# Attention scores as products of rounded parts for batches 1 to 7, plain float32 for batch 0

## The chip, the cores and the metric

The kernel runs on one core of one Trainium2 chip. The metric is device time in microseconds (us), the median of several executions; lower is better. The engines are PE (TensorE, matmuls; its weight loads are listed as PEld), DVE (VectorE), ACT (ScalarE), POOL (GpSimd) and SP (SyncE, which here issues every DMA).

## What is computed

Sparse attention over q, k, v of shape (8 batches, 8 heads, 576 rows, 64), then a gated feed-forward network (FFN) with a 3-tap convolution along the rows:

```
scores = (1/8) * q @ k^T                       # (8, 8, 576, 576)
scores = where(scores >= rowmax - tau, scores, -1e9)
attn   = exp(scores - rowmax) / (sum + 1e-9)
x      = (attn @ v), heads side by side        # (8, 576, 512)
h      = relu(x @ w_in)                        # (8, 576, 1024)
gate   = sigmoid(conv3(h, conv_w))             # along the rows
out    = (h * gate) @ w_out                    # (8, 576, 512)
```

Scores near the threshold decide which entries stay, so they are needed at float32 accuracy. The weights come as float64.

## The kernel before

**Units.** Two heads make a pair (4 pairs a batch). The 576 rows of q are cut into four tiles of 128 and one of 64. A unit is one tile of one pair, both heads: 20 units a batch, 160 in all. Each batch is handled as two chunks, tiles 0 and 1 (`g == 0`) and tiles 2 to 4 (`g == 1`), and each chunk goes through its four pairs.

**A unit, step by step** (`unit`, L335; `transposes`, L406; `attend`, L457). The scores of a head go to a PSUM tile `ps_s` (two buffers) as two blocks of 288 keys. k lies turned in SBUF as `ks`, with keys 0 to 351 of a head on partitions 0 to 63 and keys 288 to 639 on partitions 64 to 127 (the first 64 keys are repeated at the end); q is there twice, once in each half. Each of the two matmuls of a head (L355) therefore uses one half of PE's rows. For the tile of 64 rows both heads share one `ps_s` tile, so four matmuls use four quarters. DVE takes the row maximum (L364), ACT the exponential into `em` (L370, four buffers), DVE masks and sums (L373), small instructions prepare the reciprocal (L367 to L396, DVE or POOL), and POOL normalizes `em` (L401). PE transposes `em` in blocks of 128 (L420; L444 for halves), ACT copies them to `eT` (L414, two buffers, one a pair and chunk), and PE multiplies them with v into `pa` (L466). ACT and DVE split `pa` into a rounded part and a remainder (L474, L477).

**FFN.** `mm1` (L496) and `mm2` (L561) multiply in F32R, a float32 that has been rounded for PE: every operand is a rounded part (ACT copy into an F32R tile) and a remainder (a subtraction on POOL or DVE, L227), and three products are summed. `gh` and `gl` (L540, L227) are the two parts of the FFN's hidden values.

**Preparation.** `prep` (L595) loads, for each pair, `ks` (L319, and L320 multiplies it by 1/8 on ACT; once a batch), q (L327) and v (L332). It is called at a pair's first unit, for the next pair.

**Order.** Nothing is scheduled by the compiler. Each operation is given to `Plan` with an engine, an estimated duration in ns and a rank: the number of its unit minus a lead (`AHEAD`: 4.5 units for scores, 4.0 transposes, 3.5 `pa`, 5.5 preparation and 2 more for its DMAs, 0 for the FFN). `Plan.run` (L74) plays the estimates through: an engine that is free takes the ready operation of lowest rank, provided that a buffer of its tile is free, and this order is what each engine's queue gets. An operation with `other` may go to a second engine when the first one's backlog is over `BACKLOG`. For a score block of PE the estimate is 490, for the 1/8 `act(n)` = 0.833 n + 93, for a subtraction on POOL `pool(n)` = 2.1 n + 150.

## Time and profile before

| | us |
|---|---|
| median of 3 runs | 1017.34 (1016.53 to 1019.24) |
| the profiled execution: time | 1015.53 |
| the profiled execution: span, first to last instruction | 1013.7 |
| PE busy / weight loads | 973.3 / 688.9 |
| DVE, ACT, POOL busy | 766.4, 623.1, 561.4 |

The profile is one execution. A view names an instruction by its line in the kernel (L355), engine, operation and tiles (out<-in), with the shape and the count; "idle before" is the time its engine had nothing to do just ahead of it, and the arrow names what ended that. The timeline lists instructions by start; neighbours of the same line and tiles are merged (x4), and their length is from the first start to the last end. PE's ends are modelled and overlap with the next start, so distances between starts are what to read. PE's shape 64*128 means 64 rows and 128 columns of the array.

### The profile page before, as it was taken

The numbers are of one execution on the slowest core, as the hardware profiler recorded it, in microseconds if no ns is written. First come the engines' busy times: TensorE is split into PE (matmuls) and PEld (weight loads), VectorE is DVE, ScalarE is ACT, GpSimd is POOL, SyncE is SP. The second block draws the span as 40 slices with busy tenths as digits, with TensorE's granted clock in tenths as the row PEclk, the third lists the DMA queues.
The fourth block names the chain that finished last, engine by engine and source line by source line (L and its number), as shares of the span: only waits on it lengthen the run. The fifth ranks groups of instructions, "written<-read, shape, count | busy, mean of one in ns | idle before, by whom it ended". The sixth has DMA issues, their size and how long they took to land.

```text
span 1013.7 us, 18810 instructions
## 1 busy us (share of the span) xinstructions
PE 973.3 (96%) x6368; PEld 688.9 (68%) x6368; DVE 766.4 (76%) x1984; ACT 623.1 (61%) x1375; POOL 561.4 (55%) x1028
## 2 busy tenths in 40 slices
PE   5797878999999999999999999999999999999998
PEld 3464545766777677767677767776777767777786
DVE  5989998767778678886868768977687767896543
ACT  5677675665656566666656556766565655675442
POOL 3567665644556456754556536575455645584343
PEclk9899898999999999999999999999999999999999
DMA  5434243122212212212222221221222121210000
GB/s 167 123 118 125 88 117 92 43 84 72 61 52 67 71 59 63 68 57 79 61 63 64 74 61 58 67 62 64 71 63 78 49 72 38 86 34 31 22 22 31
DMA packets 41407, 70.44 MB, mean 69 GB/s; under 512 B 3936, under 2 KB 20320, under 8 KB 41312
## 3 DMA queue, kind: packets, MB, share of 16 engines
q1 hardware_dynamic: 41312, 69.25, 22.5%
q8 instruction: 51, 0.84, 0.4%
q14 instruction: 44, 0.36, 0.1%
HBM read 59.79 MB, written 9.44 MB: 68 GB/s over the span
## 4 chain that ended last, share of the span: by engine, by line
PE 83%; DVE 8%; POOL 3%; issue 2%; ACT 2%; DMA 1%; POOLq 0%; SPq 0%; ACTq 0%; DVEq 0%
PE ph L496 20%; PE po L561 18%; PE ps_s L355 16%; PE pa L466 14%; PE ps_t L420 14%; DVE few L364 2%; DVE em L373 2%; POOL em L401 2%; DMA stage<-in_w_in_dram 1%; DVE stage L265 1%; PE ps_t L444 1%; DVE stage L269 1%; POOL gl L227 1%; DVE t L523 1%; POOL t L514 1%
## 5 line engine op out<-in xcount | busy, mean ns | idle before, releaser
L401 POOL TENSOR_SCALAR em<-em,few 128x576 f32<-128x576 f32 x288 | 260.5, 911 | 77.5 <-DVE few L396 58.2
L364 DVE TENSOR_REDUCE few<-ps_s 128x1 f32<-128x576 f32 x288 | 213.6, 751 | 110.9 <-PE ps_s L355 109.6
L370 ACT ACTIVATE em<-ps_s,few 128x576 f32<-128x576 f32 x288 | 212.1, 742 | 84.8 <-DVE few L364 70.7
L373 DVE SCALAR_TENSOR_TENSOR em<-ps_s,few,em 128x576 f32<-128x576 f32 x288 | 231.9, 812 | 34.7 <-ACT em L370 30.6
L496 PE MATMUL ph<-x,w1h 128*128 128x322 f32 (+1 forms) x1024 | 255.9, 315 | 0.0
L414 ACT ACTIVATE eT<-ps_t 128x512 f32<-128x512 f32 (+1 forms) x448 | 198.6, 477 | 74.9 <-PE ps_t L420 72.0
L355 PE MATMUL ps_s<-ks,q 64*128 64x288 f32 (+1 forms) x1280 | 207.8, 451 | 25.1 <-DVE em L373 14.9
L420 PE MATMUL ps_t<-ident,em 128*128 128x128 f32 x1280 | 206.8, 285 | 9.8 <-POOL em L401 7.7
L420 PEld LDWEIGHTS ps_t<-ident,em 128*128 128x128 f32 x1280 | 149.5, 143 | 80.6 <-issue 25.8
L496 PEld LDWEIGHTS ph<-x,w1h 128*128 128x128 f32 x1024 | 177.3, 189 | 35.9 <-issue 26.3
L523 DVE SCALAR_TENSOR_TENSOR t<-hp,cw,t 128x255 f32<-128x255 f32 (+1 forms) x256 | 157.6, 618 | 29.7 <-POOL t L514 27.1
L466 PE MATMUL pa<-eT,v 128*64 128x256 f32 (+1 forms) x1280 | 171.6, 414 | 0.4 <-ACT eT L414 0.4
L496 PE MATMUL ph<-x,w1l 128*128 128x322 f32 (+1 forms) x512 | 152.2, 297 | 0.1
L355 PEld LDWEIGHTS ps_s<-ks,q 64*128 64x128 f32 (+1 forms) x1280 | 90.6, 178 | 87.7 <-issue 42.0
L466 PEld LDWEIGHTS pa<-eT,v 128*64 128x64 f32 x1280 | 86.8, 138 | 72.7 <-issue 7.6
L227 POOL TENSOR_TENSOR gl<-t,gh 128x321 fp32r<-128x321 f32 (+13 forms) x184 | 120.2, 664 | 28.2 <-ACT gh L540 27.1
L561 PE MATMUL po<-w2h,gh 128*128 128x512 f32 x288 | 122.7, 426 | 0.7 <-ACT gh L540 0.7
L514 POOL TENSOR_SCALAR t<-hp,cw 128x321 f32<-128x321 f32 (+1 forms) x128 | 72.2, 565 | 89.8 <-ACT hp L511 85.2
L367 POOL TENSOR_SCALAR few<-few,tau_sb 128x1 f32<-128x1 f32 x106 | 39.1, 369 | 135.7 <-DVE few L364 119.7
L561 PE MATMUL po<-w2h,gl 128*128 128x512 f32 x288 | 113.7, 395 | 0.5 <-POOL gl L227 0.3
L561 PE MATMUL po<-w2l,gh 128*128 128x512 f32 x288 | 113.6, 394 | 0.2 <-POOL w2l L227 0.2
L496 PEld LDWEIGHTS ph<-x,w1l 128*128 128x128 f32 x512 | 97.0, 190 | 0.9 <-POOL w1l L227 0.5
(47 smaller groups left out, 805.9 us busy)
## 6 DMA issues: line engine op xcount, KB each, us to landing
v<-in_vc_dram SPq DMA_DIRECT2D x64, 320.0 KB, 3.0
ks<-in_kd_dram SPq DMA_DIRECT2D x32, 352.0 KB, 3.6
q<-in_qd_dram SPq DMA_DIRECT2D x32, 320.0 KB, 3.3
out_dram<-ot SPq DMA_DIRECT2D x36, 256.0 KB, 2.0
q<-in_qd_dram SPq DMA_DIRECT2D x32, 256.0 KB, 3.1
stage<-in_w_in_dram SPq DMA_DIRECT2D x16, 256.0 KB, 3.3
stage<-in_w_out_dram SPq DMA_DIRECT2D x16, 256.0 KB, 2.9
stage_c<-in_conv_w_dram SPq DMA_DIRECT2D x1, 24.0 KB, 6.8
```

The lines of the kernel that those rows point to most:

```text
L227: engines[e].tensor_tensor(dst, x, y, op=ALU.subtract)
L355: nc.tensor.matmul(ps[r * n:(r + 1) * n, c, :CH], lhsT=q[rows, j, o:o + n], rhs=k[rows, j, r * D:r * D + CH], start=True, stop=True)
L364: nc.vector.tensor_reduce(few[:rows, nm], ps[:rows, :, :CH], op=ALU.max, axis=mybir.AxisListType.XY, negate=True)
L370: nc.scalar.activation(view(), ps[:rows, :, :CH], AF.Exp, bias=few[:rows, nm])
L373: nc.vector.scalar_tensor_tensor(view(), ps[:rows, :, :CH], few[:rows, th], view(), op0=ALU.is_ge, op1=ALU.mult, accum_out=few[:rows, total])
L401: engines[e].tensor_scalar(sl, sl, few[:rows, 6 + h:7 + h], few[:rows, 8 + h:9 + h], op0=ALU.mult, op1=ALU.add)
L414: "act", act(w, True), lambda dst=dst, src=src: nc.scalar.activation(dst(), src(pt), AF.Copy),
L420: nc.tensor.transpose(out=pt[:, i * P:(i + 1) * P], in_=em[:, (b0 + i) * P:(b0 + i + 1) * P], identity=ident[:])
L466: nc.tensor.matmul(pa[j * D:(j + 1) * D, :w], lhsT=vt[:, blk + j, :], rhs=eT[:, blk, :w], start=(r == 0), stop=(r == 4))
L496: nc.tensor.matmul(ph[:, :an], lhsT=w1[w][:, cb, fs], rhs=xs[cb][:, h, :an], start=(cb == 0 and i == 0), stop=(cb == NCB - 1 and i == 2))
L523: nc.vector.scalar_tensor_tensor(t[:, :kn], hp[:, k:kn + k], cw[:, 3 * f + k:3 * f + k + 1], t[:, :kn], op0=ALU.mult, op1=ALU.add)
L561: nc.tensor.matmul(po[:], lhsT=x[:, f, at:at + P], rhs=w[:, f, :], start=(f == 0 and i == 0), stop=(f == NFB - 1 and i == 2))
```

## The change

For batch 0 (`plain(b)`) the scores stay as they are: two float32 matmuls on row halves, with k and q loaded for each head by itself.

For batches 1 to 7 each head's k is loaded whole on both halves of the partitions (576 columns for the first head of a pair, 640 for the second), multiplied by 1/8 (ACT), copied to an F32R tile, which rounds it (ACT), and in the lower half of the partitions (64 to 127) the rounded value is replaced by the remainder (POOL, or DVE). q, which lies on both halves already, is split into `q1`, rounded, and `q2`, the remainder. A matmul over all 128 rows of `q1` with `ks` then gives q1 k1 + q1 k2, one of `q2` gives q2 k1 + q2 k2, and their sum is the score: four F32R matmuls a head, two for each block of 288 keys. For the tile of 64 rows the second head is multiplied first, over 128 columns (its neighbour rows in q come along), and the first head then writes rows 0 to 63 anew with 64 columns: eight matmuls.

Beside it: `em` has 3 buffers instead of 4, `eT` 1 instead of 2; preparation is called for each head j, at the first and at the second unit of the pair before; the estimate of a score block is 700 (plain) or 560 a head; k on the host is laid out like q.

```diff
@@ -313,32 +313,74 @@
     ring = [const(f"g{i}", [P, NFB, RING], F32R) for i in "hl"]
-    def prep_k(b, p):
-        ks = plan.buf(wk, "ks", 5, [P, 2, CH + D], F32, f"ks_{b}_{p}")
-        op("sp", 1000, lambda: nc.sync.dma_start(ks[:], kd[b, p]), w=[(ks, 0)], ahead=AHEAD["prep"] + 2)
-        op("act", act(2 * (CH + D)), lambda: nc.scalar.activation(ks[:], ks[:], AF.Copy, scale=0.125), w=[(ks, 0)], ahead=AHEAD["prep"])
+    def plain(b):
+        return b == 0
+    def prep_k(b, p, j):
+        n = f"{b}_{p}_{j}"
+        w = S + j * D
+        a = AHEAD["prep"]
+        if plain(b):
+            ks = plan.buf(wk, f"ks{j}", 5, [P, w], F32, f"ks_{n}")
+            cut = CH + D
+            for c in range(2):
+                rows, at = slice(c * D, (c + 1) * D), c * CH
+                m = min(cut, w - at)
+                op(
+                    "sp", 500, lambda rows=rows, at=at, m=m: nc.sync.dma_start(ks[rows, :m], kd[b, p, rows, j, at:at + m]),
+                    w=[(ks, c)], ahead=a + 2
+                )
+            cut = CH + j * D
+            op("act", act(cut), lambda: nc.scalar.activation(ks[:, :cut], ks[:, :cut], AF.Copy, scale=0.125), w=[(ks, 0), (ks, 1)], ahead=a)
+            return ks
+        xk = plan.buf(wk, "xk", 2, [P, S + D], F32, f"xk_{n}")
+        ks = plan.buf(wk, f"ks{j}", 5, [P, w], F32R, f"ks_{n}")
+        op("sp", 820, lambda: nc.sync.dma_start(xk[:, :w], kd[b, p, :, j, :w]), w=[(xk, 0)], ahead=a + 2)
+        op("act", act(w), lambda: nc.scalar.activation(xk[:, :w], xk[:, :w], AF.Copy, scale=0.125), w=[(xk, 0)], ahead=a)
+        op("act", act(w), lambda: nc.scalar.activation(ks[:], xk[:, :w], AF.Copy), w=[(ks, 0), (ks, 1)], r=[(xk, 0)], ahead=a)
+        op(
+            "pool", pool(w), lambda e: subtract(e, ks[D:], xk[D:, :w], ks[D:].bitcast(F32)),
+            w=[(ks, 0), (ks, 1)], r=[(xk, 0)], ahead=a, other=[("dve", dve(w))]
+        )
         return ks
-    def prep_q(b, p, g):
+    def prep_q(b, p, j, g):
         o, w = NEW[g]
-        q = plan.buf(wk, "q", 3, [P, 2, w], F32, f"q_{b}_{p}_{g}")
-        op("sp", 900, lambda: nc.sync.dma_start(q[:], qd[b, p, :, :, o:o + w]), w=[(q, 0)], ahead=AHEAD["prep"] + 2)
-        return q
+        n = f"{b}_{p}_{j}_{g}"
+        src = qd[b, p, :, j, o:o + w]
+        a = AHEAD["prep"]
+        if plain(b):
+            q1 = plan.buf(wk, "q1", 4, [P, w], F32, f"q1_{n}")
+            op("sp", 455, lambda: nc.sync.dma_start(q1[:], src), w=[(q1, 0)], ahead=a + 2)
+            return [q1]
+        xq = plan.buf(wk, "xq", 2, [P, w], F32, f"xq_{n}")
+        q1 = plan.buf(wk, "q1", 4, [P, w], F32R, f"q1_{n}")
+        q2 = plan.buf(wk, "q2", 4, [P, w], F32R, f"q2_{n}")
+        op("sp", 455, lambda: nc.sync.dma_start(xq[:], src), w=[(xq, 0)], ahead=a + 2)
+        op("act", act(w), lambda: nc.scalar.activation(q1[:], xq[:], AF.Copy), w=[(q1, 0)], r=[(xq, 0)], ahead=a)
+        op(
+            "pool", pool(w), lambda e: subtract(e, q2[:], xq[:], q1[:].bitcast(F32)),
+            w=[(q2, 0)], r=[(xq, 0), (q1, 0)], ahead=a, other=[("dve", dve(w))]
+        )
+        return q1, q2
     def load_v(b, p, g):
         vt = plan.buf(wk, "v", 2, [P, NBLK + 1, D], F32, f"v_{b}_{p}_{g}")
         op("sp", 820, lambda: nc.sync.dma_start(vt[:], vc[b, p]), w=[(vt, 0)], ahead=AHEAD["prep"])
         return vt
-    def unit(u, k, q, o, n):
+    def unit(u, kt, qt, o, n):
         heads = [[0, 1]] if 2 * n <= P else [[0], [1]]
         m, rows = len(heads), n * len(heads[0])
-        em = plan.buf(wk, "em", 4, [P, 2 * S], F32, f"em_{u}")
+        em = plan.buf(wk, "em", 3, [P, 2 * S], F32, f"em_{u}")
         few = plan.buf(sm, "few", 4, [P, 10], F32, f"few_{u}")
         a = AHEAD["s"]
@@ -348,14 +390,25 @@
             nm, th, total = (slice(at + h, at + h + 1) for at in (0, 2, 4))
             def mm(js=js, ps=ps):
-                for r, j in enumerate(js):
+                if len(qt[0]) == 1:
+                    for r, j in enumerate(js):
+                        for c in range(2):
+                            on = slice(c * D, (c + 1) * D)
+                            nc.tensor.matmul(
+                                ps[r * n:(r + 1) * n, c, :CH], lhsT=qt[j][0][on, o:o + n], rhs=kt[j][on, r * D:r * D + CH],
+                                start=True, stop=True
+                            )
+                    return
+                for r, j in reversed(list(enumerate(js))):
                     for c in range(2):
-                        rows = slice(c * D, (c + 1) * D)
-                        nc.tensor.matmul(
-                            ps[r * n:(r + 1) * n, c, :CH], lhsT=q[rows, j, o:o + n], rhs=k[rows, j, r * D:r * D + CH],
-                            start=True, stop=True
-                        )
+                        at = r * D + c * CH
+                        for i in range(2):
+                            nc.tensor.matmul(
+                                ps[:(r + 1) * n, c, :CH], lhsT=qt[j][i][:, o - r * n:o + n], rhs=kt[j][:, at:at + CH],
+                                start=(i == 0), stop=(i == 1)
+                            )
             def view(h=h):
                 return em[:rows, h * S:(h + 1) * S].rearrange("p (a b) -> p a b", a=2)
@@ -376,7 +429,8 @@
                 )
             op(
-                "pe", 490, mm, w=[(ps, 0)], r=[(k, 0), (q, 0)], ahead=a
+                "pe", 560 * len(js) if len(qt[0]) > 1 else 700, mm, w=[(ps, 0)],
+                r=[(kt[j], i) for j in js for i in range(2)] + [(x, 0) for j in js for x in qt[j]], ahead=a
             )
             op("dve", 665, top, w=[(few, ("nm", h))], r=[(ps, 0)], ahead=a)
             op("act", 624, exp, w=[(em, h)], r=[(ps, 0), (few, ("nm", h))], ahead=a)
@@ -592,17 +646,19 @@
     units = [(i, t) for i in range(len(pairs)) for t in GROUPS[pairs[i][0] % 2]]
     kss, qss, vts, ems, eTs = {}, {}, {}, {}, {}
-    def prep(i):
+    def prep(i, j):
         if i >= len(pairs):
             return
         c, p = pairs[i]
         b, g = chunks[c]
         if g == 0:
-            kss[b, p] = prep_k(b, p)
-        qss[i] = prep_q(b, p, g)
-        vts[i] = load_v(b, p, g)
-    prep(0)
+            kss[b, p, j] = prep_k(b, p, j)
+        qss[i, j] = prep_q(b, p, j, g)
+        if j == 0:
+            vts[i] = load_v(b, p, g)
+    for j in range(2):
+        prep(0, j)
     load_conv()
     for i in range(W1N + W2N):
@@ -616,10 +672,10 @@
             c, p = pairs[i]
             b, g = chunks[c]
             n = TILES[t][1]
-            em = unit(now, kss[b, p], qss[i], TILES[t][0] - NEW[g][0], n)
+            em = unit(now, [kss[b, p, j] for j in range(2)], [qss[i, j] for j in range(2)], TILES[t][0] - NEW[g][0], n)
             w = NEW[g][1]
             if t == GROUPS[g][0]:
-                eT = plan.buf(wk, "eT", 2, [P, NBLK, 320], F32, f"eT_{i}")
+                eT = plan.buf(wk, "eT", 1, [P, NBLK, 320], F32, f"eT_{i}")
             transposes(now, em, n, eT, TILES[t][0] - NEW[g][0])
             if t == GROUPS[g][-1]:
                 x = plan.buf(wk, f"x{g}", NP, [P, 2, COLS[g][1]], F32R, f"x{g}_{i}")
@@ -633,7 +689,9 @@
                     )
                 attend(i, eT, vts[i], w, x, off)
             if t == GROUPS[g][0]:
-                prep(i + 1)
+                prep(i + 1, 0)
+            if t == GROUPS[g][1]:
+                prep(i + 1, 1)
             if t == GROUPS[g][-1] and p == NP - 1:
                 seq = ffn(c)
@@ -666,15 +724,13 @@
         x = np.asarray(x).reshape(B, H // 2, 2, -1, D).transpose(0, 1, 4, 2, 3)
         return np.concatenate([x, x], axis=2)
-    turned = np.concatenate([np.asarray(k), np.asarray(k)[:, :, :64]], axis=2)
-    turned = turned.reshape(B, H // 2, 2, S + 64, D).transpose(0, 1, 2, 4, 3)
     blocks = np.asarray(v).reshape(B, H // 2, 2 * S // 128, 128, D)
     middle = np.zeros((B, H // 2, 2, 128, D), np.float32)
     middle[:, :, 0, :64] = blocks[:, :, 4, :64]
     middle[:, :, 1, 64:] = blocks[:, :, 4, 64:]
     ins = {
         'qd': doubled(q),
-        'kd': np.stack([turned[..., :S // 2 + 64], turned[..., S // 2:]], axis=2).transpose(0, 1, 2, 4, 3, 5).reshape(B, H // 2, 2 * D, 2, -1),
+        'kd': doubled(np.concatenate([np.asarray(k), np.asarray(k)[:, :, :64]], axis=2)),
         'vc': np.concatenate([blocks[:, :, :4], middle, blocks[:, :, 5:]], axis=2).transpose(0, 1, 3, 2, 4),
         'tau': np.asarray(tau).reshape(1, 1),
         'w_in': np.asarray(moe_w_in).view(np.int64),
```

## The prediction

> **What bounds the kernel now.** I read the page's busy times first, then the table of windows, PE's waits in the middle window, and last the timeline of PE alone, because the score matmuls are what the change rewrites.
>
> ```profile
> span 1013.7 us, 18810 instructions
> ...
> PE 973.3 (96%) x6368; PEld 688.9 (68%) x6368; DVE 766.4 (76%) x1984; ACT 623.1 (61%) x1375; POOL 561.4 (55%) x1028
> ...
> 200.00:950.00 750.00, 748.91 (x5021) 535.35 (x5019) 567.41 (x1469) 467.55 (x1029) 415.13 (x764) 1.00 0.21 62
> ...
> PE ps_t L420 <- POOL em L401: 0.8, 3, 0.3
> PE ps_t L420 <- POOL hp L508: 0.3, 1, 0.3
> ```
>
> Columns of the third line: window, length, then busy us of PE, PEld, DVE, ACT and POOL, the granted clock (1.00), DMA share and GB/s. PE is busy 748.9 of 750 us, and the two wait rows are all that PE waited for there: 1.1 us. The other 39 of its 40.4 idle us (1013.7 - 973.3) lie before 200 us and after 950 us. In that window DVE is at 76%, ACT at 62%, POOL at 55%. So from 200 to 950 us only PE time counts; before it, PE time saved may be worth nothing.
>
> Busy does not say what a score block really takes from PE, since the matmuls overlap in their records. Starts do. Four places of PE's timeline (start, length, line, names, shape, count):
>
> ```profile
> 515.80 0.31 PE L496 MATMUL ph<-x,w1l 128*128 128x322 f32 x1
> 515.95 0.31 PE L496 MATMUL ph<-x,w1h 128*128 128x322 f32 x1
> 516.18 0.76 PE L355 MATMUL ps_s<-ks,q 64*128 64x288 f32 x4
> 516.87 0.42 PE L496 MATMUL ph<-x,w1h 128*128 128x322 f32 x1
> 517.12 0.32 PE L496 MATMUL ph<-x,w1l 128*128 128x322 f32 x1
> ```
> ```profile
> 374.59 0.28 PE L496 MATMUL ph<-x,w1h 128*128 128x256 f32 x1
> 374.71 0.60 PE L420 MATMUL ps_t<-ident,em 128*128 128x128 f32 x4
> 375.24 0.76 PE L355 MATMUL ps_s<-ks,q 64*128 64x288 f32 x4
> 375.93 0.66 PE L420 MATMUL ps_t<-ident,em 128*128 128x128 f32 x4
> 376.34 0.36 PE L496 MATMUL ph<-x,w1h 128*128 128x256 f32 x1
> ```
> ```profile
> 308.77 0.31 PE L496 MATMUL ph<-x,w1h 128*128 128x322 f32 x1
> 309.00 1.24 PE L355 MATMUL ps_s<-ks,q 64*128 64x288 f32 x8
> 310.18 0.42 PE L496 MATMUL ph<-x,w1h 128*128 128x322 f32 x1
> 310.43 0.31 PE L496 MATMUL ph<-x,w1l 128*128 128x322 f32 x1
> ```
> ```profile
> 303.34 0.31 PE L496 MATMUL ph<-x,w1h 128*128 128x322 f32 x1
> 303.58 0.71 PE L355 MATMUL ps_s<-ks,q 64*64 64x288 f32 x8
> 304.23 0.42 PE L496 MATMUL ph<-x,w1h 128*128 128x322 f32 x1
> 304.48 0.32 PE L496 MATMUL ph<-x,w1l 128*128 128x322 f32 x1
> ```
>
> The trace shows each plain float32 matmul as two records, so x4 is one head of a 128-row tile, x8 two heads, and the x8 of 64*64 both heads of a 64-row tile. Read the starts. A ph matmul of 322 columns follows another after 0.15 us (515.80 to 515.95). The last ph ahead of a score block holds PE for 0.23 (515.95 to 516.18), 0.08 more; the block of one head takes 0.69 (516.18 to 516.87); the first ph behind it takes 0.25 instead of 0.15. One head therefore costs 0.69 + 0.08 + 0.10 = 0.87 us between ph blocks. A second head in the same block adds only 0.48 (309.00 to 310.18 is 1.18, the single 0.69 with rounding). So of 0.87 us some 0.4 is the price of switching into row halves and out again. Between transposes it is much the same: four transposes ahead of the block take 0.53 (374.71 to 375.24), four behind it 0.41.
>
> **The change, part by part.** *Scores of batches 1 to 7, 128-row tiles.* Two matmuls on row halves become four over all 128 rows, in the rounded type that ph runs in. From ph's spacings, 0.12 us for 256 columns (374.59 to 374.71) and 0.15 for 322, a 288-column one takes 0.134, one head 0.54. No switch should remain: ph has the same 128*128 shape, and passing between ph and transposes costs nothing visible (the transposes start 0.12 after the ph, at its usual spacing). The saving per block:
> one head between ph: 0.87 - 0.54 = 0.33; between transposes 0.69 + 0.09 + 0.05 - 0.54, about 0.30 (0.53 against four transposes at 0.11, 0.41 against 0.36); two heads between ph: 1.18 + 0.08 + 0.10 - 1.07 = 0.29, between transposes 0.25. Beside pa less, since pa is itself of another shape (128*64):
>
> ```profile
> 509.64 2.38 PE L466 MATMUL pa<-eT,v 128*64 128x256 f32 x20
> 511.95 0.33 PE L420 MATMUL ps_t<-ident,em 128*128 128x128 f32 x1
> ```
>
> pa pays its own exit whoever follows (2.31 us for the block, before transposes as well), so a neighbouring score block shares it; I take 0.15 for one head and 0.08 for two.
>
> How many blocks lie in the saturated window:
>
> ```profile
> 200.00:950.00 750.00, 157.77 (x1016) 69.63 (x1016) 347.66 (x681) 167.26 (x227) 1.00 0.21 62
> ```
>
> These are the rows of the score tile there: 1016 matmul records, which I counted in PE's timeline as 112 blocks of one head, 44 of two and 27 of a 64-row tile (112 x 4 + 44 x 8 + 27 x 8 = 1016). That is 254 heads of 320; the 66 earlier ones are all 40 of batch 0 and 26 of batch 1, so the window is wholly changed work, and a batch takes 750 x 40 / 254 = 118 us. By neighbours: 85 singles free of pa (0.32 on average: 27.2 us), 27 beside pa or a 64-row block (0.15: 4.0), 22 pairs free (0.27: 5.9), 22 beside pa (0.08: 1.8). Sum 39 us.
>
> *64-row tiles lose.* Now both heads run at once in 64*64 quarters: 303.58 to 304.23 is 0.65, with 0.09 before and 0.10 after 0.84 us. Then there are eight full matmuls, 8 x 0.134 = 1.07: 0.23 lost. Four of the eight write 64 columns only, as pa and the quarters do; if they need the switch too, another 0.27 goes (0.09 in, 0.10 out, and a block's end of about 0.09), 0.5 in all. No row shows this shape in the rounded type; 27 x 0.23 to 0.5 is 6 to 13.5 us. I take 10: a 64-column output is what pa, the nearest row, has, but pa's switch is often shared. PE's balance: 39 - 10 = 29 us (25 to 33).
>
> *What the other engines get.* Rows of the same kind of work:
>
> ```profile
> L320 ACT ACTIVATE ks<-ks 128x704 f32<-128x704 f32 x32 | 25.3, 791 | 19.6 <-DMA ks<-in_kd_dram 19.6
> ...
> L540 ACT ACTIVATE gh<-t 128x320 fp32r<-128x320 f32 x8 | 3.7, 461 | 0.0
> L540 ACT ACTIVATE gh<-t 128x256 fp32r<-128x256 f32 x8 | 3.3, 414 | 0.0
> ...
> L227 POOL TENSOR_TENSOR gl<-t,gh 128x320 fp32r<-128x320 f32 x8 | 7.1, 889 | 0.5 <-ACT gh L540 0.5
> L227 POOL TENSOR_TENSOR gl<-t,gh 128x256 fp32r<-128x256 f32 x8 | 6.3, 794 | 0.0
> L227 POOL TENSOR_TENSOR gl<-t,gh 128x64 fp32r<-128x64 f32 x8 | 2.7, 341 | 1.6 <-ACT gh L540 1.6
> ```
>
> ACT, per batch: 4 activations of 704 go (3.2 us); for k, 8 of 576 and 8 of 640 come (0.68 and 0.74 by the slope from 320 to 704 columns: 11.4) and for q 8 of 256 and 8 of 320 (7.0): +15 us. POOL, per batch: 4 subtractions of 576, 4 of 640 (1.44 and 1.57 by the slope from 64 to 320) and 8 each of 256 and 320: 12.0 + 13.5 = +25.5 us. Over a batch of 118 - 29 / 6.35 = 113.5 us that makes ACT (467.6 / 6.35 + 15) / 113.5 = 78%, POOL (415.1 / 6.35 + 25.5) / 113.5 = 80%, DVE 567.4 / 6.35 / 113.5 = 79%. None becomes the bound by itself. All of it is hidden under PE as long as PE's order never meets a late operand; DVE at 76% leaves PE waiting 1.1 us today. Uncovered it would cost up to its own length, 6.35 x 40 us.
>
> *Cover that shrinks.* em goes from four buffers to three, eT from two to one. A unit takes 118 / 20 = 5.9 us, so three em buffers still allow 17.7 us from exp to transposes. One eT means that the next pair's transposes can't be copied out before pa has ended; at 511.95 the transposes come after pa anyway. Nothing for both, up to the price of the second rival below. The planner's prices matter more: it charges a score block 490 ns where PE needs 690 to 870, so PE runs late against the plan and everybody else comes early. The new 560 is close to 0.54. That reserve is part of why PE never waits, and it shrinks. No row prices it; between 0 and that rival's 62 us, I take 6, about 1 us a batch, nearer to zero because the row nearest to it is the 1.1 us of waiting in 750.
>
> *SP and batch 0.* SP issues 8 transfers for k and 16 for q a batch instead of 4 and 8, with v and out behind them in its one queue, and they wait for a free xk or xq. DMA share is 0.21, prep is ranked 7.5 units ahead: nothing. Batch 0 keeps its matmuls; its k comes in smaller pieces: nothing, give or take 2 us in the 200 us that PE does not fill.
>
> Sum: -29 + 6 = **-23 us**. The profiled execution took 1015.53 us (span 1013.7 and 1.8 around it); the median of the runs is 1017.34. So 992.5 against the profile and **994** against the median.
>
> **Rivals.** *The reserve is gone* (partial gain): waits of 9 to 26 us in place of my 6, 1003 to 1014. For: three engines near 80% and plan prices that now fit. Against: POOL and ACT have idle time in every unit today.
>
> *Norms come late* (slower). The norm on POOL is the last step ahead of the transposes, and it now queues behind subtractions.
>
> ```profile
> L401 POOL TENSOR_SCALAR em<-em,few 128x576 f32<-128x576 f32 x288 | 260.5, 911 | 77.5 <-DVE few L396 58.2 <-PE ps_t L420 8.7 <-PE pa L466 6.6
> ```
>
> Subtractions hold POOL 25.5 of 113.5 us, so 22% of the norms find one running, and wait for half of 1.1 us on average, or for a second one: 0.25 us for each of the 252 norms of seven batches, 62 us in all, with one em buffer fewer to absorb it. If all of it reached PE: 1017 - 29 + 62 = 1050; it decides from about half, 29 us. Against: ffn's gl work already shares that queue, and the norm's 260.5 us on POOL let 0.8 us of waiting through to PE.
>
> *The halves were worth it* (slower). If the switch belongs to plain float32 beside rounded matmuls and not to row halves, the transposes keep it alive, and only streaming is compared: 200 heads x (0.54 - 0.48) + 27 x (1.07 - 0.65) = +23 us, 1040. The Trainium skill, TensorE: Matmul & The Clock Gate, section "Why this matters for your kernels", has the same bent: it advises running small-K matmuls concurrently in separate row groups. By that rule the change gives away a factor that it should keep; the trace agrees for the second head of a block (0.48), not for a block with its ends (0.87). Against: transposes, plain float32 as well, start after ph at ph's own spacing.
>
> *No change*: gain and waits cancel within 3 us.
>
> **How the numbers follow.** Chances: forecast (982 to 1003) 0.66, partial gain (1003 to 1014) 0.13, no change 0.07, late norms 0.11, halves 0.03. 0.3% is 3 us, about what a measurement of this kernel can tell from no change. Faster 0.79, same 0.07, slower 0.14. The low end is the upper balance with no waits, 1017 - 33 = 984, and 2 for the start: 982. The high end takes in the partial gain and no change, and leaves the two slower cases out: 1018.
>
> **What would show it.** Right: score matmuls of batches 1 to 7 as x4 a head, 128*128, at 0.13 us spacing, with ph behind them at its usual 0.15; PE busy over 99% in a middle window some 25 us shorter; ACT and POOL at 76 to 82% there. Wrong: PE rows waiting for em, eT or q in the tens of us; a spacing above 0.17 in the new matmuls; 64-row tiles above 1.4 us. If the time is above 1014, a wait has taken the gain.

## The result and the profile after

The changed kernel takes 1032.07 us (median of 4 runs, 1030.21 to 1032.39); the kernel before, run beside it, 1016.93 (1016.12 to 1019.24). The ratio is 1.0141, 95% interval 1.012 to 1.0162: slower by 15 us, where 23 us faster was forecast. The profiled execution has a span of 1029.7 us against 1013.7.

The page of after (busy us, share of the span, instructions):

```profile
span 1029.7 us, 19586 instructions
...
PE 958.9 (93%) x6368; PEld 762.4 (74%) x6368; DVE 815.2 (79%) x2077; ACT 705.7 (69%) x1575; POOL 712.2 (69%) x1103
```

The windows of after, in the columns of the prediction, and then the first window of before:

```profile
0.00:200.00 200.00, 157.13 (x947) 104.34 (x948) 176.73 (x454) 136.78 (x304) 134.28 (x206) 0.91 0.39 115
...
200.00:950.00 750.00, 727.07 (x4991) 596.52 (x4990) 603.32 (x1548) 536.66 (x1195) 549.12 (x843) 1.00 0.24 71
```
```profile
0.00:200.00 200.00, 165.45 (x1027) 104.63 (x1027) 173.68 (x468) 131.86 (x288) 122.28 (x218) 0.93 0.36 111
```

PE's waits in after from 200 to 950 us (total, times, longest):

```profile
PE ps_t L474 <- POOL em L455: 16.0, 24, 1.3
PE ps_t L474 <- DVE x L531: 2.2, 5, 0.6
PE ps_s L408 <- DVE em L426: 2.1, 6, 0.7
```

PE is less busy than before (958.9 against 973.3), so the new matmuls are cheaper. But it now idles in the window that it had filled: 22.9 of 750 us, where it was 1.1. The largest wait is the transposes' for a norm on POOL, 16.0 us where it was 0.8. In the first 200 us PE does less as well (157.1 busy for 165.5, 947 matmul records for 1027), although batch 0 keeps its score matmuls.

**The new matmuls by themselves.** PE's timeline of after: a head between `ph` blocks, and a 64-row tile:

```profile
291.63 0.31 PE L550 MATMUL ph<-x,w1h 128*128 128x322 f32 x1
291.77 0.71 PE L408 MATMUL ps_s<-ks,q 128*128 128x288 f32 x4
292.32 0.32 PE L550 MATMUL ph<-x,w1h 128*128 128x322 f32 x1
292.48 0.31 PE L550 MATMUL ph<-x,w1l 128*128 128x322 f32 x1
...
315.36 0.31 PE L550 MATMUL ph<-x,w1h 128*128 128x322 f32 x1
315.51 1.22 PE L408 MATMUL ps_s<-ks,q 128*128 128x288 f32 x8
316.56 1.04 PE L474 MATMUL ps_t<-ident,em 128*128 128x128 f32 x8
```

The head takes 0.55 us (291.77 to 292.32), and the `ph` around it keep their usual 0.15: no switch is left, against 0.87 in all before. The x8 is half 128*128 and half 128*64 (timelines merge neighbours), as the view of the tile in that window shows:

```profile
L408 PE MATMUL ps_s<-ks,q x8: 292/294/296, 315.5 to 316.4; 128*128 128x288 f32 x4, 128*64 128x288 f32 x4
```

It takes 1.05 us (315.51 to 316.56), so the 64-column half pays no switch either.

**Time that PE loses.** For each pair of neighbouring matmuls I took the usual distance of their starts, and added up what exceeds it. The span less this sum is the work that PE would do unhindered.

| us | before | after |
|---|---|---|
| beyond the usual, 0 to 200 us | 51.1 | 66.0 |
| beyond the usual, from 200 us | 4.8 | 35.2 |
| span less both | 957.8 | 928.5 |

So PE's work fell by 29.3 us, and 45.3 us of loss came: 14.9 in the first 200 us, 30.4 behind them. What counts as usual moves these sums: taken over all runs and also by what stands ahead of the pair, they are 32.6 and 48.7 (16.2 and 32.5), so they are good to some 3 us. The experiments ask where these 45 us come from.

### The profile page after: what moved, and what is told of

Its sections match the earlier page's. It is cut to its first block, busy times and chain, and to the rows that moved or that the text cites. A ratio compares the mean times of both kernels' runs of the same rounds, so it can differ in the third digit from the quotient of the medians.

```text
span 1029.7 us, 19586 instructions
## 1 busy us (share of the span) xinstructions
PE 958.9 (93%) x6368; PEld 762.4 (74%) x6368; DVE 815.2 (79%) x2077; ACT 705.7 (69%) x1575; POOL 712.2 (69%) x1103
## 4 chain that ended last, share of the span: by engine, by line
PE 25%; DVE 14%; POOL 7%; ACT 4%; issue 4%; DMA 1%; POOLq 0%; ACTq 0%; DVEq 0%
PE po L615 8%; PE ps_s L408 4%; PE pa L520 4%; PE ps_t L474 4%; DVE em L426 4%; PE ph L550 4%; DVE t L577 4%; DVE few L417 3%; POOL em L455 3%; POOL gl L227 2%; DVE t L584 1%; ACT em L423 1%; POOL t L568 1%; POOL q L227 1%; ACT eT L468 1%
## 5 line engine op out<-in xcount | busy, mean ns | idle before, releaser
L455 POOL TENSOR_SCALAR em<-em,few 128x576 f32<-128x576 f32 x288 | 262.5, 918 | 66.6 <-DVE few L450 53.7
L426 DVE SCALAR_TENSOR_TENSOR em<-ps_s,few,em 128x576 f32<-128x576 f32 x288 | 231.0, 811 | 33.7 <-ACT em L423 30.9
L550 PE MATMUL ph<-x,w1h 128*128 128x322 f32 (+1 forms) x1024 | 247.0, 308 | 0.8 <-ACT hp L565 0.8
L468 ACT ACTIVATE eT<-ps_t 128x512 f32<-128x512 f32 (+1 forms) x448 | 198.8, 477 | 48.7 <-PE ps_t L474 47.1
L408 PE MATMUL ps_s<-ks,q 128*128 128x288 f32 (+1 forms) x1120 | 194.4, 307 | 10.9 <-DVE em L426 10.2
L577 DVE SCALAR_TENSOR_TENSOR t<-hp,cw,t 128x255 f32<-128x255 f32 (+1 forms) x256 | 175.7, 690 | 33.3 <-POOL t L568 18.0
L408 PEld LDWEIGHTS ps_s<-ks,q 128*128 128x128 f32 (+1 forms) x1120 | 158.8, 185 | 28.6 <-issue 11.7
L520 PE MATMUL pa<-eT,v 128*64 128x256 f32 (+1 forms) x1280 | 175.0, 421 | 0.6 <-ACT eT L468 0.6
L568 POOL TENSOR_SCALAR t<-hp,cw 128x321 f32<-128x321 f32 (+1 forms) x128 | 74.8, 585 | 58.6 <-ACT hp L565 52.6
L227 POOL TENSOR_TENSOR q<-xq,q 128x256 fp32r<-128x256 f32 (+1 forms) x112 | 93.6, 843 | 28.8 <-ACT q L365 19.6
```

The costliest lines, as they stand in the source:

```text
L227: engines[e].tensor_tensor(dst, x, y, op=ALU.subtract)
L408: nc.tensor.matmul(ps[:(r + 1) * n, c, :CH], lhsT=qt[j][i][:, o - r * n:o + n], rhs=kt[j][:, at:at + CH], start=(i == 0), stop=(i == 1))
L426: nc.vector.scalar_tensor_tensor(view(), ps[:rows, :, :CH], few[:rows, th], view(), op0=ALU.is_ge, op1=ALU.mult, accum_out=few[:rows, total])
L455: engines[e].tensor_scalar(sl, sl, few[:rows, 6 + h:7 + h], few[:rows, 8 + h:9 + h], op0=ALU.mult, op1=ALU.add)
L468: "act", act(w, True), lambda dst=dst, src=src: nc.scalar.activation(dst(), src(pt), AF.Copy),
L520: nc.tensor.matmul(pa[j * D:(j + 1) * D, :w], lhsT=vt[:, blk + j, :], rhs=eT[:, blk, :w], start=(r == 0), stop=(r == 4))
```

## The experiments

The matmul term stood. Four readings of the loss could be told apart: the smaller buffers; the new *order* (a plan with more work in it); POOL's *time* (its norms queue behind the subtractions); and *holding* (a POOL instruction that runs keeps a DVE instruction from finishing, or the other way round). All ratios are to the kernel before, with their 95% interval. Lines differ between kernels: the tap of the convolution is L523 before and L577 after, the gate L530 and L584, the norm L401 and L455.

### Buffers alone, in the kernel before (b_buf)

```diff
-        em = plan.buf(wk, "em", 4, [P, 2 * S], F32, f"em_{u}")
+        em = plan.buf(wk, "em", 3, [P, 2 * S], F32, f"em_{u}")
...
-                eT = plan.buf(wk, "eT", 2, [P, NBLK, 320], F32, f"eT_{i}")
+                eT = plan.buf(wk, "eT", 1, [P, NBLK, 320], F32, f"eT_{i}")
```

> The kernel before with em at 3 buffers and eT at 1, nothing else. Theory A (the subtractions on POOL delay the norms and hold up VectorE): the buffers are not the cause, 1017 +- 4 us, PE waits from 200 to 950 us stay under 5 us. Theory B (the smaller buffers take the cover away): PE waits for transposes as in the changed kernel; most of the 45 us of added PE waits appears without the 29 us saved in matmuls, 1040 to 1062 us. Theory C (the planner's new prices and a plan that now fits too tightly): 1017 +- 4.

1017.03 us, 1.0005 (0.9993 to 1.0017). In the kernel before, the buffers cost nothing.

### The subtractions as a load on the kernel before (b_load)

For batches 1 to 7, subtractions of the change's sizes into scratch; the scores stay as they are.

```diff
+        if b:
+            for j in range(2):
+                n = S + j * D
+                dk = plan.buf(wk, "dk", 1, [P, S + D], F32R, f"dk_{b}_{p}_{j}")
...
+                op("pool", pool(n), load, w=[(dk, 0)], r=[(ks, 0)], ahead=AHEAD["prep"], other=[("dve", dve(n))])
```

> The kernel before with added work that nothing reads: for batches 1 to 7 the same 168 subtractions on POOL as in the change (64 partitions by 576 and 640 columns for k, 128 by 256 and 320 for q), from ks and q into a scratch tile, at the same rank. Scores stay plain float32. Theory A: VectorE's instructions with two operands from SBUF get longer (taps of 321 columns from 646 to about 740 ns on average), norms come late, PE waits; since PE is slower than in the changed kernel part is absorbed: 1025 to 1045. Theory B and C: POOL has room (55 to 73 percent busy), 1017 +- 4.

1039.83 us, 1.0223 (1.0203 to 1.0244). The added subtractions alone cost 23 us without the new matmuls, though they take 149 us of POOL where the change's take 181. Most of it is lost early: the score matmul that starts at 225 us before starts 17.5 us later here, and the last ones 25 us later. Behind that PE, with its dearer score blocks, waits hardly more than before (0.7 us for norms from 200 to 930).

### The change without subtractions (a_nosub)

Both subtractions are gone: k's lower half stays rounded and q's rounded part is used twice, so the remainders are left out of the scores (and the rounded product counts four times).

```diff
-        op(
-            "pool", pool(w), lambda e: subtract(e, ks[D:], xk[D:, :w], ks[D:].bitcast(F32)),
-            w=[(ks, 0), (ks, 1)], r=[(xk, 0)], ahead=a, other=[("dve", dve(w))]
-        )
...
-        return q1, q2
+        return q1, q1
```

> The changed kernel without the subtractions: k keeps its rounded value in both halves and q's rounded part is used in place of its remainder, so the remainders are left out of the scores; matmuls, loads, ACT copies, buffers and prices stay. Theory A: PE's waits go and the matmuls' gain shows, 985 to 998. Theory B: waits stay, 1025 to 1032. Theory C: POOL's part goes but the tight plan stays, 1010 to 1025.

988.72 us, 0.9721 (0.9701 to 0.9742): the forecast without its 6 us of waits (1017 - 29 = 988). Everything else that the change does (ACT's added work, SP's transfers, the buffers, the plan's new prices) costs nothing that shows. The whole loss hangs on the subtractions.

### All subtractions on DVE (a_dve)

```diff
-            "pool", pool(w), lambda e: subtract(e, ks[D:], xk[D:, :w], ks[D:].bitcast(F32)),
-            w=[(ks, 0), (ks, 1)], r=[(xk, 0)], ahead=a, other=[("dve", dve(w))]
+            "dve", dve(w), lambda: subtract("dve", ks[D:], xk[D:, :w], ks[D:].bitcast(F32)),
+            w=[(ks, 0), (ks, 1)], r=[(xk, 0)], ahead=a
```

(and the same for q)

> The changed kernel with all subtractions given to VectorE. Theory A: POOL's norms are on time again, but VectorE gets 14 us a batch more (about 90 percent busy) and its two-operand work still meets POOL's; the early stretch, where VectorE is full, loses more: 1025 to 1045. Theory B: norms do not matter, the smaller buffers do: 1030 +- 5, about the changed kernel. Theory C: 1030 to 1045.

1027.8 us, 1.0108 (1.009 to 1.0126), with DVE busy 628.2 of 730 us from 200 to 930. Moving the work changes little: PE's transposes still wait 15.2 us for norms there, presumably because DVE's maxima and sums, which the norms need, now stand behind the subtractions.

### One-operand load on the kernel before (b_load1)

As b_load, with multiplications by 1 in place of the subtractions, sized to hold POOL about as long (158 us in all, for 149):

```diff
-                    subtract(e, dk[D:, :n], x, x)
+                    m = {576: 524, 640: 605}[n]
+                    for _ in range(2):
+                        engines[e].tensor_scalar(dk[D:, :m], x[:, :m], 1.0, 1.0, op0=ALU.mult, op1=ALU.mult)
```

> The kernel before with the same occupation of POOL as in the run with 168 added subtractions, at the same ranks and planned costs, but from instructions with one tensor operand and constants (multiplications by 1 into a scratch tile that nothing reads). Theory A1 (VectorE's instructions with two SBUF operands cannot run beside POOL's with two): no exclusion, so VectorE's taps keep their length and the time stays at 1017 to 1022. Theory A2 (the norms queue behind the added work on POOL, whatever it is): the loss of 23 us stays, 1035 to 1042.

1033.7 us, 1.0164 (1.0144 to 1.0185). It was meant to keep POOL's time and take the holding away, and did not: taps that begin beside such a multiplication are longer by the time it has left, less 0.2 us (correlation 0.98 and 1.0 for k's and q's). One operand holds DVE as two do, so this run separates nothing.

### Subtractions in pieces (a_split)

```diff
+        for i in range(4):
+            at = slice(i * w // 4, (i + 1) * w // 4)
+            op(
+                "pool", pool(w // 4), lambda e, at=at: subtract(e, ks[D:, at], xk[D:, at], ks[D:, at].bitcast(F32)),
+                w=[(ks, i % 2)], r=[(xk, 0)], ahead=a, other=[("dve", dve(w // 4))]
+            )
```

(q in two pieces likewise)

> The changed kernel with each subtraction for k in four pieces and each for q in two, on the same engine; the work is the same plus a fixed 0.15 us for each of the 280 added instructions. A1: what VectorE waits for is the rest of the running piece, at most 0.5 instead of 1.5 us; of the 45 us of added waits a third to a half goes, 1010 to 1022. A2: POOL has 42 us more work and nothing gets better, 1030 to 1040.

1023.62 us, 1.0071 (1.005 to 1.0092): 8 us better than after. Presumably shorter instructions let norms in between and hold DVE for less; the pieces' own starts raise POOL's busy time from 712 to 759 us.

### No subtraction for k (a_nosubk)

k's remainder is left out; q is split as in the change.

> The changed kernel without the subtractions for k: both halves keep k's rounded part, so k's remainders are left out of the scores; q is still split. Waits for a running instruction go with the square of its length: 56 of 1.43 and 1.57 us against 112 of 0.79 and 0.89 us is 126 to 79. A1: some 60 percent of the 43 us between the changed kernel and the one without subtractions comes back, 1002 to 1010. A2 goes by the time held, 86 to 94 us: about half, 1008 to 1014.

1001.86 us, 0.9861 (0.9833 to 0.9888). k's subtractions account for 30 of the 43 us between this series' ends (988.7 and 1032.1), q's for the other 13, though they hold POOL for about as long. POOL's groups in after:

```profile
L227 POOL TENSOR_TENSOR ks<-xk,ks 64x640 fp32r<-64x640 f32 x28 | 46.0, 1641 | 2.0
L227 POOL TENSOR_TENSOR ks<-xk,ks 64x576 fp32r<-64x576 f32 x28 | 41.7, 1488 | 4.6 <-ACT ks L344 2.4
L227 POOL TENSOR_TENSOR q<-xq,q 128x320 fp32r<-128x320 f32 x56 | 50.0, 900 | 18.9 <-ACT q L365 9.8 <-PE ps_s L408 8.0 <-DVE few L450 0.8
L227 POOL TENSOR_TENSOR q<-xq,q 128x256 fp32r<-128x256 f32 x56 | 43.6, 786 | 9.9 <-ACT q L365 9.8
```

k: 87.7 us in 56 instructions of 1.5 to 1.6 us; q: 93.6 us in 112 of 0.8 to 0.9. The long ones cost more than their share, with one reservation: k was removed first, while both loads were there, and the second of two loads may cost more than the first.

### Batches 0 and 1 plain (a_plain2)

```diff
-        return b == 0
+        return b <= 1
```

> The changed kernel with batches 0 and 1 plain instead of batch 0 alone. By the starts of the scores, 14 us of the loss arise before 250 us, while VectorE is full with the weights, and none after. If the subtractions for batch 1 meet the weights there, 1016 to 1023; if the early loss comes from smaller buffers or prices, 1030 +- 3.

1021.83 us, 1.0046 (1.0029 to 1.0062), 10 us better than after. In the first 250 us, where the weights are prepared on the same engines, the subtractions buy less than they cost.

### POOL held by memsets, kernel before (b_memset)

As b_load, with memsets in place of the subtractions (169 us on POOL, for 149). A memset reads nothing.

```diff
-                    subtract(e, dk[D:, :n], x, x)
+                    for m in (640, 640) if n == 576 else (640, 640, 180):
+                        engines[e].memset(dk[:, :m], 0.0)
```

> The kernel before with POOL held for about the same time as in the two runs with added work, at the same ranks and planned costs, but by memsets of a scratch tile, which read nothing. A1 (VectorE's two-operand instructions wait for POOL's running instruction): memsets of one column showed no such wait before; if longer ones show none either, taps of 321 columns stay near 650 ns and the time is 1017 to 1022. A2 (the added work delays POOL's own work, the norms): 1033 to 1040 as with the other added work.

1031.43 us, 1.0135 (1.0091 to 1.0179). Taps beside a memset are not longer (-2 and -4 ns in the middle of 10 and 33 cases), so a load that doesn't hold DVE exists. It costs 14 us here, b_load 23: the taps came out as A1 has it, the time nearer to A2's.

### The added operations in the plan alone, kernel before (b_noop)

As b_memset, with memsets of one column and the plan's prices kept: the order stays, POOL's time goes.

```diff
-                    for m in (640, 640) if n == 576 else (640, 640, 180):
+                    for m in (1,):
```

> The kernel before with the added operations of the earlier load runs still in the plan at full planned cost, but each issuing only a memset of one column. So every engine's order is that of the load runs, and POOL's time is not. O (the changed order in the early stretch costs the time): 1028 to 1034, as with the memsets. A2 (POOL's time itself, its own work comes late): 1017 +- 4.

1021.08 us, 1.0039 (1.0025 to 1.0052). With b_memset and b_load, the kernel before pays some 4 us for the order, 10 for POOL's time, 9 for the holding. The last two are good to 5 us only: b_memset's four runs lie between 1026 and 1037 us, and it kept POOL busy for 20 us more than b_load.

### The order of the change alone (a_noop)

Subtractions of one column, at their full price in the plan; q's rounded part is used twice, so the remainders are left out.

```diff
-            "pool", pool(w), lambda e: subtract(e, ks[D:], xk[D:, :w], ks[D:].bitcast(F32)),
+            "pool", pool(w), lambda e: subtract(e, ks[D:, :1], xk[D:, :1], ks[D:, :1].bitcast(F32)),
...
-            "pool", pool(w), lambda e: subtract(e, q2[:], xq[:], q1[:].bitcast(F32)),
+            "pool", pool(w), lambda e: subtract(e, q2[:, :1], xq[:, :1], q1[:, :1].bitcast(F32)),
```

> The changed kernel with its order kept: the subtractions are planned at full cost but work on one column; the scores take q's rounded part twice, so the remainders are left out. O: the early loss of some 14 us stays and the waits after 200 us go, 1000 to 1005. A1 and A2: all of the 43 us goes, as without subtractions, 986 to 992.

986.45 us, 0.9702 (0.9684 to 0.972). In the changed kernel the order costs nothing, nor do the 38.5 us that the one-column subtractions still take on POOL.

### The order and POOL's time, without the holding (a_memset)

Memsets in the subtractions' places, 177 us in all for their 181; the remainders are zeros.

```diff
-            "pool", pool(w), lambda e: subtract(e, ks[D:], xk[D:, :w], ks[D:].bitcast(F32)),
+            "pool", pool(w), lambda e: [engines[e].memset(ks[D:, :m].bitcast(F32), 0.0) for m in (w, w, 200 if w == S else 330)],
```

(and the same for q with `(w, w, w // 6)`)

> The changed kernel in its own order, with memsets in place of the subtractions that hold POOL for about the same time (0.75 to 1.6 us each); the remainders are then zero, so they are left out of the scores. Long memsets did not lengthen VectorE's taps. A1 (exclusion of VectorE): PE's waits from 200 to 950 us fall from 33 to about 10, 1003 to 1012. A2 (POOL's own work comes late): the waits stay near 30, 1025 to 1033.

1008.0 us, 0.991 (0.9892 to 0.9927). That splits the loss. From a_noop to a_memset the ratio rises by 0.0208, 21 us: POOL's time. From a_memset to after by 0.0231, 24 us: the holding. Together 45 us, all of it; each part is good to some 3 us. The windows from 200 to 930 us, of a_noop, a_memset and after:

```profile
200.00:930.00 730.00, 726.11 (x5054) 604.79 (x5054) 571.81 (x1549) 537.94 (x1196) 420.17 (x834) 1.00 0.24 71
```
```profile
200.00:930.00 730.00, 716.75 (x4948) 592.04 (x4945) 564.93 (x1528) 530.84 (x1182) 527.23 (x1116) 1.00 0.23 71
```
```profile
200.00:930.00 730.00, 707.07 (x4856) 579.63 (x4855) 587.74 (x1508) 523.18 (x1163) 534.96 (x817) 1.00 0.25 72
```

PE falls in two steps of some 10 us. In the first, POOL (fifth figure) rises from 420 to 527 and DVE (third) doesn't; in the second POOL rises by 8 only, and DVE is 23 us busier with 20 instructions fewer. PE's wait for the norm goes the same way, in a_noop and then a_memset (after: 16.0, all within this window):

```profile
PE ps_t L474 <- POOL em L455: 1.5, 3, 0.7
```
```profile
PE ps_t L474 <- POOL em L455: 9.3, 20, 0.9
```

So 7.8 of the first 9.4 us that PE loses in this window, and 6.7 of the second 9.7, are transposes waiting for a norm: both parts reach PE mostly there. In the first 200 us it is another wait that grows with the holding, that of score matmuls for the mask on DVE which frees `ps_s`: 14.1 us in a_noop, 12.4 in a_memset, 18.1 in after (for batch 0's, then batch 1's):

```profile
PE ps_s L397 <- DVE em L426: 10.0, 8, 3.5
PE ps_s L408 <- DVE em L426: 8.1, 9, 1.9
```

How one held instruction looks, DVE's timeline and then POOL's, of after:

```profile
445.41 1.58 DVE L584 SCALAR_TENSOR_TENSOR t<-t,hp 128x321 f32<-128x321 f32 x1
446.91 0.15 DVE L443 TENSOR_SCALAR few<-few 128x2 f32<-128x2 f32 x1
```
```profile
445.23 1.41 POOL L227 TENSOR_TENSOR ks<-xk,ks 64x576 fp32r<-64x576 f32 x1
446.74 0.65 POOL L568 TENSOR_SCALAR t<-hp,cw 128x321 f32<-128x321 f32 x1
```

The gate at 445.41 needs 0.49 us alone. POOL's subtraction ends at 446.64 (445.23 + 1.41), and the gate at 446.99, 0.35 behind it: it stood for 1.09 us. Behind it in DVE's queue stands L443, part of the reciprocal for which a norm waits. Over the trace, taps and gates that begin beside a subtraction of k are longer by the time it has left, less 0.20 (12 taps) or 0.14 us (7 gates), correlation 1.00. It works the other way as well: k's subtractions take 1.43 and 1.57 us in the middle case, but most of those that begin while a tap or gate runs are longer, up to 1.73 and 1.87. The groups show DVE's side too, before, after and a_memset:

```profile
L523 DVE SCALAR_TENSOR_TENSOR t<-hp,cw,t 128x321 f32<-128x321 f32 x128 | 82.4, 646 | 20.2 <-POOL t L514 18.2 <-POOL hp L508 1.6
...
L269 DVE SCALAR_TENSOR_TENSOR stage<-stage 128x256 uint32<-128x256 uint32 x32 | 16.2, 511 | 0.0
```
```profile
L577 DVE SCALAR_TENSOR_TENSOR t<-hp,cw,t 128x321 f32<-128x321 f32 x128 | 94.0, 737 | 17.2 <-POOL t L568 15.2 <-POOL hp L560 1.2 <-POOL hp L562 0.4
...
L426 DVE SCALAR_TENSOR_TENSOR em<-ps_s,few,em 128x576 f32<-128x576 f32 x288 | 231.0, 811 | 33.7 <-ACT em L423 30.9 <-POOL hp L562 0.5 <-POOL few L420 0.4
...
L269 DVE SCALAR_TENSOR_TENSOR stage<-stage 128x256 uint32<-128x256 uint32 x32 | 21.1, 659 | 0.0
```
```profile
L577 DVE SCALAR_TENSOR_TENSOR t<-hp,cw,t 128x321 f32<-128x321 f32 x128 | 83.4, 654 | 20.6 <-POOL t L568 16.7 <-POOL hp L560 1.8 <-POOL hp L562 1.6
```

The mean tap went from 646 to 737 ns, and with memsets is back at 654. The mask and sum, L426, has one operand in PSUM and isn't touched (811; 812 before, as L373). The weights' step L269 grew from 511 to 659 ns (4.9 us in its 32 instructions; 554 with memsets), which falls into the first 200 us. The trace agrees with the Trainium skill, SBUF — State Buffer, section "SBUF: two separate sides": a port pair that DVE and POOL share goes to one instruction at a time, whole, and a DVE operation with two inputs in SBUF stands against a POOL operation that reads SBUF. That rule speaks against this change, and the prediction did not weigh it.

### k's remainder on DVE, q's on POOL in halves (c1)

The 1/8 goes into the rounding (one ACT pass less for each k), batches 0 and 1 are plain, and q's subtraction is split as in a_split.

```diff
+            "dve", dve(w), lambda: nc.vector.scalar_tensor_tensor(
+                ks[D:], xk[D:, :w], 0.125, ks[D:].bitcast(F32), op0=ALU.mult, op1=ALU.subtract
+            ),
```

> A version from what the runs showed: batches 0 and 1 plain; k is rounded with the 1/8 in the same ACT instruction, its remainder comes from one VectorE instruction that multiplies by 1/8 and subtracts (0.75 to 0.82 us); q's remainder stays on POOL in two pieces. A1: no instruction of over 0.6 us is added to POOL, ACT loses 5.7 us a batch; VectorE gets 6.3 us a batch. 1008 to 1018. A2: POOL loses 12 us a batch, 1010 to 1018.

1011.37 us, 0.9937 (0.992 to 0.9953). POOL's long subtractions are gone, DVE has their work instead: faster than both kernels, with about a fifth of the matmul gain left.

### k of both heads at once (c2), and batch 1 plain too (c2p)

In the change, 128 partitions hold one head's k twice, and only the lower half's remainder is used. Here they hold both heads of a pair once: one rounding (with the 1/8) and one remainder of 640 columns for the pair, and four DMAs within SBUF put the parts in their places.

```diff
+        op("act", act(w), lambda: nc.scalar.activation(hk[:], x(), AF.Copy, scale=0.125), w=[(hk, 0)], r=[(xk, 0)], ahead=a)
+        op(
+            "dve", dve(w), lambda: nc.vector.scalar_tensor_tensor(xk[:], x(), 0.125, y(), op0=ALU.mult, op1=ALU.subtract),
+            w=[(xk, 0)], r=[(hk, 0)], ahead=a
+        )
...
+                    "sp", 500, lambda h=h, ks=ks, part=part, at=at, dst=dst: nc.sync.dma_start(
+                        ks[dst].bitcast(F32), part[at, :S + h * D].bitcast(F32)
+                    ),
```

> The changed kernel with k split for both heads of a pair at once: head 0 on partitions 0 to 63, head 1 on 64 to 127, one ACT rounding (with the 1/8) and one VectorE remainder of 640 columns a pair instead of four ACT copies and two POOL subtractions, the parts then placed by four SBUF to SBUF DMAs. q as in the change, batch 0 plain. By the run without k's subtractions (1001.9) plus 3.3 us a batch on VectorE: 1002 to 1012 if the DMAs come in time, over 1020 if the scores wait for them.

1014.56 us, 0.9977 (0.9964 to 0.999), above the range of 1002 to 1012.

> The same with batches 0 and 1 plain. The early loss is mostly gone without k's subtractions on POOL, and batch 1 gives up its gain in the part after 200 us (about 2.5 us): 1003 to 1013.

1001.47 us, 0.9843 (0.9825 to 0.986): 16 us faster than the kernel before and 31 faster than the change. Its page, and its window from 200 to 930 us:

```profile
span 999.4 us, 19581 instructions
...
PE 944.4 (94%) x6368; PEld 745.1 (75%) x6368; DVE 793.7 (79%) x2045; ACT 655.3 (66%) x1479; POOL 642.9 (64%) x1087
...
200.00:930.00 730.00, 716.74 (x4960) 587.61 (x4960) 585.12 (x1501) 494.15 (x1111) 491.04 (x822) 1.00 0.29 81
```

PE is at 716.7, as in a_memset, not at the 726 of a_noop; q's subtractions are still on POOL, which is the likely cause. Batch 1 plain is worth 13 us here, the start again.

### q of both heads at once as well (c4)

c2p with one rounding and one subtraction for q of a pair, and eight more DMAs within SBUF.

> The version with k split for both heads at once and batches 0 and 1 plain, with q done the same way: one ACT rounding and one POOL subtraction for each pair and chunk instead of two, and eight SBUF to SBUF DMAs that put the parts in place. POOL has 6.7 us a batch less and ACT 3.5 us. SP issues 64 DMAs a batch more, about 0.5 us each, in one queue. If they come in time 994 to 1000; if scores wait for q, 1005 to 1030.

1027.76 us, 1.0111 (1.0089 to 1.0133), a miss. POOL's busy time falls to 604.9 us, yet the time rises by 26. POOL's waits and then ACT's, from 200 to 940 us:

```profile
POOL xq L227 <- ACT hq L386: 51.0, 27, 5.9
```
```profile
ACT hq L386 <- DMA xq<-in_qd_dram: 30.8, 20, 3.2
```

A late transfer holds ACT's rounding, that holds POOL's subtraction at the head of its queue for up to 5.9 us, and the norms stand behind it; PE waits 15.6 us for them. SP's queue shows two reasons (L399 places q's parts, L385 loads `xq`):

```profile
SPq L399 <- PE ps_s L447: 132.9, 51, 11.7
SPq L385 <- DMA q<-xq: 39.1, 30, 2.3
```

Placements stand at the head of the one queue until scores leave a buffer of q free, and loads stand until the transfers out of the single `xq` have landed. What each of the two costs, no run tells.

## Why the prediction was wrong

**PE bounds the middle, not the start**: right. In a_noop, where PE is 99% busy from 200 to 930 us, the saving on matmuls comes out whole.

**The matmuls**: right. 0.55 us for a head between `ph`, forecast 0.54; PE's work fell by 29.3 us, forecast 29 (that they agree to less than the 3 us of the method is luck). The same sum, span less lost time, is 927.9 for a_noop and 928.0 for a_memset: these two and after differ in PE's waits alone. The 64-row tile came out at the lower bound (1.05 us, no switch).

**"The halves were worth it"** fell with that, and with it, for this case, the bent of the Trainium skill's page TensorE: Matmul & The Clock Gate ("Why this matters for your kernels") toward row groups: 0.87 us by halves, 0.55 whole. No run has the rounded matmuls by halves, so whether the switch belongs to the halves or to plain float32 stays open.

**The lengths on POOL**: right (1.49 and 1.64 us, forecast 1.44 and 1.57). **SP, the buffers, ACT**: nothing, as said. **The plan's new prices**, for which above all the 6 us stood: nothing either. a_noop has all of these.

**"All of it is hidden under PE as long as PE's order never meets a late operand", and 6 us for the rest**: this step failed. It measured 45, and the sign that the prediction gave for it came: PE's rows wait 16.0 us for `em`. The evidence for the 6 was that PE waited 1.1 us in 750 with DVE at 76%, and that three engines would stay near 80%. Neither says how much more a chain bears: exp, sums, reciprocal and norm pass through ACT, DVE and POOL in turn, and a unit's delay there can be one instruction's length, whatever the share. The first half of the loss is the rival "norms come late": right in place (transposes waiting for POOL's `em`), at 21 us instead of 62, and below its own point of 29.

**What no rival had** is the other half. The prediction added POOL's work to POOL alone. But a POOL subtraction also stops DVE's taps, gates and weight steps, and they stop it: 24 us, and the reason why the loss passed 29.

**Batch 0: "nothing, give or take 2 us in the 200 us that PE does not fill"**: failed, 14.9 us. DVE is the busiest engine there (173.7 of 200 us before), and its weight steps are among those held. What costs is less batch 0's own loads than batch 1's subtractions, which are already made then: with batch 1 plain, 10 us come back (a_plain2). Of the 14.9, a_memset still has 4.3 (55.4 against 51.1), and a_noop has -4.1.

**Left open**: the split between time and holding is measured, and so is where PE waits in the end (for norms in the middle, for masks too at the start). Which held instructions make those norms and masks late, reciprocals behind held taps or POOL's own instructions, is not.

## What to carry to other kernels

Before work is moved to an engine with idle time, ask whose chain its queue serves and what its running instruction stops elsewhere: the price is the length of one added instruction at the wrong moment, not its share of the busy time. Two cheap runs tell the parts of such a loss apart: the added operations cut to one column (order alone), and replaced by memsets of the same time (order and queue, nothing held). Where an operand must be split, split it once for all its users and let DMA place the parts, as c2p does, but keep the transfers out of the way of the engine that feeds the norms, as c4 did not.

## What the runs showed of the hardware

A one-operand multiplication on POOL holds DVE's two-operand instructions just as a subtraction does; a memset of the same length doesn't (-2 ns). Norms on POOL, which scale by a value for each partition, hold DVE too, and DVE holds them. Of the 75 taps in after that began beside a norm, 55 had less than 0.7 us of it left; 53 of these were longer by that time less 0.2 us, or not at all where less was left (correlation 0.98). The other 20 had 1.0 us or more left and were not longer (21 ns at most), but there the norm took 1.06 to 1.55 us, where 0.82 is usual. In the first group the norm was ahead and the tap stood, in the second the tap was ahead and the norm stood.
